# Attention and a two-layer feed-forward block on one core: output weights in 8 KB runs, a stepped weight load, one reciprocal DMA a head, WI in four pieces

## The chip, the core and the metric

The kernel runs on one core of a Trainium2 chip. The metric is device time in microseconds (us): the median of three runs. A separate execution was profiled; all rows of the profile come from that one. Engines are named as in the profile: PE (matrix multiply) with PEld (its weight loads), DVE (vector), ACT (activation), POOL (GpSimd), SP (which issues most DMAs here). SPq is SP's instruction queue; POOL issues DMAs too, those that convert from float32 to float16.

## The reference

Eight batches, eight heads, 576 positions, head dimension 64. Each head has a coarse attention over means of four positions and a local attention over positions less than four apart; their sum goes through a feed-forward block of 512 to 2048 to 512 with an ELU between.

```python
q_d, k_d, v_d = (t.reshape(B, H, Sd, 4, D).mean(axis=3) for t in (q, k, v))
out_up = np.repeat(sm_attn(q_d, k_d, v_d), 4, axis=2)
mask = np.abs(pos[:, None] - pos[None, :]) < 4
...                                      # softmax of the masked scores
out_local = np.matmul(attn, v)
attn_out = out_up + out_local
...
x = attn_out.transpose(0, 2, 1, 3).reshape(B * S, H * D)      # 4608 x 512
h = x @ w_in                                                  # w_in 512 x 2048
g = np.where(h > 0.0, h, np.exp(np.minimum(h, 0.0)) - 1.0)
out = g @ w_out                                               # w_out 2048 x 512
```

## The kernel before

**Attention.** The heads go in pairs, so that two heads of 64 fill 128 partitions; there are four pairs a batch, index `j`. For each pair PE transposes q and k, makes local scores in six blocks of 96 positions and coarse scores beside them; ACT takes the exponential into a tile `pex`; POOL casts v to float16 (line 226). `outputs` (line 536) multiplies by v into a PSUM tile `lg`. `normalise` has DVE multiply `lg` by the reciprocals of the softmax sums, `rcb`, into `ln` (line 554 in batches 0 to 2; lines 558 and 561 after that), and adds the local part and the coarse part, repeated four times, into `xt`: the transposed input of the feed-forward block, 512 tokens a tile. Most of these additions are POOL's (line 574).

**Reciprocals.** For batches 1 to 7, `denominators(b)` collects all softmax sums of a batch in one PSUM bank: 32 rows for each pair `j`, of which ten are used. A matmul with a window of the constant `IND` as its weights chooses the row; the windows start at column `a`. Before, rows 0 to 3 hold the local sums of the pair's first head, 144 positions a row, rows 4 to 7 those of its second head, row 8 the coarse sums of the first and row 9 of the second. DVE takes the reciprocal into `rc`. Each reciprocal is then needed on 64 partitions. In batches 1 and 2 (`spread_four`) PE does that, with the constant `FOUR`. In batches 3 to 7 `spread_out` writes `rc` to a DRAM tile `rd`, and `spread_in` (line 466) reads it back with a step of zero over 64 partitions: for each head `e` one DMA of the local part (4 x 144 numbers a pair) and one of the coarse part (144), four a batch, on SP's queue.

**Feed-forward.** `WI` holds w_in as 128 partitions x 4 blocks of rows x 2048 columns, `WO` holds w_out as 128 x 16 x 512. For a token tile `t` and a block `fc` of 128 of the 2048 hidden units, `mm1` (line 592) makes `hp` with four matmuls, each with 128 columns of WI as weights and 512 tokens moving. ACT takes the exponential (line 597), DVE finishes the ELU in two steps (`e`, line 598; `gt`, line 601). `mm2` (line 615) uses `gt` as weights and WO as the moving operand, sums over all 16 blocks, and ACT copies the result out (line 621). In `mm1` and `mm2` there are nine token tiles, 16 steps each, four matmuls a step. The first two blocks of the first tile are made ahead of that by `ahead` (line 793), as soon as each pair of heads is done.

**Loads.** WI comes in five DMAs on POOL's queue (`load_wi`, line 138): columns 0 to 256, 256 to 512, and then 512 at a time. WO comes in four DMAs of four row blocks (`load_wo`, line 142); a row of w_out is 2 KB in DRAM and 1 KB once converted. POOL also issues q and k of batches 0 and 1 (line 152). SP issues v (line 204), and q and k of later batches (line 170).

**Order.** Nothing is scheduled automatically. Every step is put into a list with a planned time by `at`, the list is sorted, and the steps are emitted in that order; each engine works its own steps off in that order, waiting where an operand is not there. The times of the front are in the table `F` (planned times of the WI loads: `wi`), those of later batches in `PLAN`, `LATER` and `LAST`. POOL's order in the front therefore interleaves DMA issues, casts of v, and additions into `xt`.

Of the kernel before, what the change touches and what calls it, by code (L numbers as in the profile page):

```python
# [15 lines left out]
B, H, S, D = 8, 8, 576, 64  # L16
SD = S // 4
# [9 lines left out]
NPAIR = H // 2  # L27
RW = S + SD
# [5 lines left out]
I1 = 31  # L34
# [34 lines left out]
def _free(ap: bass.AP, dims) -> bass.AP:  # L69

    return bass.AP(tensor=ap.tensor, offset=ap.offset, ap=[list(ap.ap[0])] + [list(d) for d in dims])
# [3 lines left out]
def kernel(  # L75
# [9 lines left out]
    nc = tc.nc  # L85
# [26 lines left out]
    def bank(tag, name):  # L112
        pool = late["ps"] if tag == "hp" else ps
        return pool.tile([128, 512], FP32, tag=tag, bufs=2, name=name)
# [16 lines left out]
    C = {}  # L131
    WI = sb.tile([128, DMC, DFF], FP16, tag="WI", bufs=1, name="WI")
    WO = sb.tile([128, FCN, DM], FP16, tag="WO", bufs=1, name="WO")
    KT = [sb.tile([128, S + 2 * KO], FP16, tag=f"kt{i}", bufs=1, name="kt") for i in range(3)]

    def load_wi(a, z):
        src = moe_w_in.rearrange("(c p) m -> p c m", p=128)[:, :, a:z]
        nc.gpsimd.dma_start(out=WI[:, :, a:z], in_=src)

    def load_wo(n):  # L140
        src = moe_w_out.rearrange("(c p) m -> p c m", p=128)[:, 4 * n : 4 * n + 4, :]
        nc.gpsimd.dma_start(out=WO[:, 4 * n : 4 * n + 4, :], in_=src)

    KD = [sb.tile([128, 2 * KG + 16], FP16, tag=f"kd{i}", bufs=1, name="kd") for i in range(3)]
# [270 lines left out]
    def local(b, j, e, g, a, n):  # L415
        return st[(b, j)]["p"][:, e, g, a : a + n]

    def far(b, j, e, kg, a, n):
        return st[(b, j)]["p"][0:KG, e, kg, HB + a : HB + a + n]
# [11 lines left out]
    def denominators(b):  # L431


        den = bank("hp" if b < 3 else "misc", "den")
        for r in range(8):
            a = 126 if r == 0 else I1 - r
            for j in range(NPAIR):
                nc.tensor.matmul(
                    den[32 * j : 32 * j + 32, 0:SD], C["IND"][:, a : a + 32],
                    local(b, j, r // 4, r // 2 % 2, SD * (r % 2), SD),  # L440
                    start=(r == 0), stop=False, tile_position=(0, 32 * j),
                )
        for e in range(2):
            a = 63 + I1 - 8 - e
            for kg in range(2):
                for j in range(NPAIR):
                    nc.tensor.matmul(
                        den[32 * j : 32 * j + 32, 0:SD], C["IND"][0:KG, a : a + 32],
                        far(b, j, e, kg, 0, SD), start=False,
                        stop=(e == 1 and kg == 1), tile_position=(0, 32 * j),  # L450
                    )
        rc = RC[b] = sb.tile([128, SD], FP16, tag="rc", bufs=1, name="rc")
        nc.vector.reciprocal(out=rc[:], in_=den[:, 0:SD])
# [7 lines left out]
    def spread_in(b):  # L461
        rd = RD[b]
        rcb = RB[b] = sb.tile([128, NPAIR, RW], FP16, tag="rcb", bufs=2, name="rcb")
        for e in range(2):
            for r, a, n in ((4 * e, 0, S), (8 + e, S, SD)):
                nc.sync.dma_start(
                    out=rcb[64 * e : 64 * e + 64, :, a : a + n],
                    in_=bass.AP(
                        tensor=rd.tensor, offset=rd.offset + r * SD,
                        ap=[[0, 64], [32 * SD, NPAIR], [1, n]],  # L470
                    ),
                )


    def den_pair(b, j, den):
# [48 lines left out]
    xts = {}  # L524
# [59 lines left out]
    def mm1(t, fc):  # L584
        if fc == 0:
            gts[t] = sb.tile([128, FCN, TBLK], FP16, tag="gt", bufs=2, name="gt")
        if t == 0 and fc < 2:
            hp = FS.pop(fc)[:]
        else:
            hp = bank("misc" if t == 0 and fc % 2 else "hp", "hp")[:]  # L590
            for dc in range(DMC):
                nc.tensor.matmul(  # L592
                    hp, WI[:, dc, 128 * fc : 128 * fc + 128], xts[t][:, dc, :],
                    start=(dc == 0), stop=(dc == DMC - 1),
                )
        e = sb.tile([128, TBLK], FP16, tag="e", bufs=3, name="e")
        nc.scalar.activation(out=e[:], in_=hp, func=AF.Exp)  # L597
        nc.vector.tensor_scalar(  # L598
            out=e[:], in0=e[:], scalar1=1.0, scalar2=-1.0, op0=AB.min, op1=AB.add
        )  # L600
        nc.vector.scalar_tensor_tensor(  # L601
            out=gts[t][:, fc, :], in0=hp, scalar=0.0, op0=AB.max, in1=e[:], op1=AB.add
        )
# [24 lines left out]
    Z = fs.tile([128, 512], FP16, tag="Z", bufs=1, name="Z")  # L628
# [96 lines left out]
    def selections(name):  # L725

        if name == "SEL":
            t = C[name] = sb.tile([KW, 1280], FP16, tag=name, bufs=1, name=name)
            src, parts = C["ID"], ((0, 6, 0), (6, 4, 32))
            step = 64  # L730
        else:
            src = sb.tile([KW, 10], FP16, tag="I4", bufs=1, name="I4")
            nc.vector.tensor_reduce(
                out=src[:], in_=_free(C["ID"][:, 0:1], [[1, 10], [32, NPAIR]]), axis=AX.X, op=AB.add
            )
            t = C[name] = sb.tile([KW, 640], FP16, tag=name, bufs=1, name=name)
            parts, step = ((0, 4, 0), (4, 1, 8)), None
        for n, m, col in parts:
            nc.gpsimd.tensor_copy(
                out=t[:, 128 * n : 128 * n + 128 * m].rearrange("p (n e d) -> p n e d", e=2, d=64),  # L740
                in_=_free(src[:, col : col + 1], [[1, m], [step or (4 if m > 1 else 1), 2], [0, 64]]),
            )

    FS = {}
# [43 lines left out]
    def ahead(dc):  # L788

        for fc in range(2):  # L790
            if dc == 0:
                FS[fc] = bank("hp", "hp")
            nc.tensor.matmul(
                FS[fc][:], WI[:, dc, 128 * fc : 128 * fc + 128],
                xts[0][:, dc, :], start=(dc == 0), stop=(dc == 3),
            )

# [6 lines left out]
    def at(time, fn, *args):  # L804
        events.append((time, len(events), fn, args))
# [30 lines left out]

    at(-100, first)
    at(-65.22, second)
    F = dict(T=[-39.33, -39.15, -31.04, -21.56], S=[-39.11, -32.34, -29.72, -11.12], Z=[-38.51, -29.77, -26.1, -10.33], C=[-30.42, -27.74, -25.81, -9.49], V=[-12.6, -10.91, -10.66, -8.84], P=[-20.39, -13.26, -9.3, -7.53], O=[-10.7, -10.4, -9.52, -5.16], N=[-9.74, -9.71, -7.85, -0.84], H=[-8.39, -5.24, -0.57, -0.51], lv=[-32.55, -28.19, -28, -27.16], cv=[-27.16, -11.94, -11.66, -10.33], lw=[-11.12, -10.26, -8.16, 0.45], rp=[-40.13, -31.28, -14.21, -9.89], D=[-27.94, -26.42, -12.68, -9.32], wi=[-30.86, -13.56, -10.44, -4.62, 0.11], cf=[-9.53], k=[-39.29, -38.62, -33.61, -32.56, -31.33])
    FK = dict(Tq=[0, 0, 0, 0], Tk=[3, 0, 0, 0], S=[2, 0, 0, 1], Z=[0, 0, 0, 1], P=[0, 0, 0, 0], O=[0, 0, 1, 1], D=[0, 0, 0, 1])  # L840
    for j in range(NPAIR):
        at(F["T"][j], first_transposes, j, (FK["Tq"][j], FK["Tk"][j]))
        at(F["S"][j], first_scores, j, 0, FK["S"][j])
        at(F["Z"][j], first_scores, j, 1, FK["Z"][j])
        at(F["D"][j], first_dens, j, FK["D"][j])
        at(F["V"][j], first_v, j)
        at(F["P"][j], first_spread, j, FK["P"][j])
        at(F["O"][j], first_outputs, j, FK["O"][j])
        at(F["N"][j], first_normalise, j)
        at(F["H"][j], ahead, j)  # L850
        at(F["lv"][j], load_v, 0, j)
        at(F["cv"][j], cast_v, 0, j)
        at(F["lw"][j], load_v, 1, j)
        at(F["rp"][j], run_pair, 1, j)
    for x, a, z in zip(F["wi"], (0, 256, 512, 1024, 1536), (256, 512, 1024, 1536, 2048)):
        at(x, load_wi, a, z)
    at(F["cf"][0], close_front)
    late_consts = (("VR", vr_np), ("IND", ind_np), ("SEL", None), ("QI", qi_np), ("FOUR", None))
    for x, (name, a) in zip(F["k"], late_consts):
        if a is None:  # L860
            at(x, selections, name)
        else:
            at(x, const, a, name, nc.sync)
# [9 lines left out]
    def mm1_at(t, i):  # L873
        a, d = MM1[t] if t < 4 else (MM1[3][0] + 16 * (t - 3), 1)
        return a + d * i
# [19 lines left out]
    for b in range(4, B):  # L895
        z = mm1_at(b, 0)
        PLAN[b] = {k: [z + x for x in a] for k, a in (LATER if b < B - 1 else LAST).items()}
    for b in range(1, B):
        p = PLAN[b]
        for j in range(NPAIR):  # L900
            n = NPAIR * (b - 2) + j
# [28 lines left out]
    for n, x in enumerate([-3.64, 3.75, 7.34, 13.63]):  # L930
        at(x, load_wo, n)
    for t in range(NT):
        for i in range(16):
            at(mm1_at(t, i), mm1, t, i)
            if 16 * t + i <= 16 * NT - 4:
                at(mm2_at(t, i), mm2, t, i)
# [32 lines left out]
```

## Time and profile before

| | us |
|---|---|
| median of 3 runs | 371.23 |
| lowest and highest of them | 369.82, 371.39 |
| the profiled execution | 368.46 |
| its span, first to last instruction | 366.7 |
| PE busy | 343.6 |
| DVE busy | 244.2 |
| ACT busy | 201.0 |
| POOL busy | 146.7 |

The mean granted TensorE clock is 0.986 of full speed. DMA moved 49.15 MB in 132,099 packets, of which 7,664 (6.26 MB, 11.3% of the time of 16 DMA engines) came from POOL's software queue and 123,946 (41.93 MB, 52.6%) from SP's hardware queue. A row of a group gives the line, engine, operation, tiles and shapes, the number of instructions, then busy us and mean ns of one, then the idle time of the engine just before them and what ended it. PE's and PEld's rows overlap: a matmul's length in a group includes its way through the array, so the distance of one start from the next is shorter.

### The profile page before, as it was taken

What the parts mean: (1) busy time and instruction counts of PE and PEld (TensorE: products, weight loads), DVE (VectorE), ACT (ScalarE), POOL (GpSimd) and SP (SyncE); (2) the same over time, 40 slices, a digit from 0 to 9 for tenths busy, and PEclk for the clock granted to TensorE, in tenths of its full rate; (3) what the DMA queues carried; (4) which work ended last, traced back from release to release, by engine and by line L of the source; (5) the groups of instructions that cost most, each with busy time, mean ns of one, the idle gap of its engine ahead of it and who ended that gap; (6) DMA issues with size and microseconds to landing.
All of it is one profiled execution on the core that took longest, in us unless ns stands there. A gap on an engine that the chain in (4) does not pass through costs nothing.

```text
span 366.7 us, 8593 instructions
## 1 busy us (share of the span) xinstructions
PE 343.6 (94%) x3432; PEld 177.6 (48%) x3432; DVE 244.2 (67%) x451; ACT 201.0 (55%) x321; POOL 146.7 (40%) x264
## 2 busy tenths in 40 slices
PE   6995989999789999999999989999999999999996
PEld 3773444544444455455445444544454444444443
DVE  2059478756777777987799779868865865555510
ACT  3854586357963764667367736773664344344321
POOL 8296363399437912780297029703500410000000
PEclk9999699999998999999999999999999999999999
DMA  9999968999995869497949594914103101001012
GB/s 173 210 172 195 171 101 163 217 236 265 227 156 120 173 158 198 46 229 172 206 109 221 142 217 104 229 45 105 47 30 95 49 29 59 29 29 59 29 57 88
DMA packets 132099, 49.15 MB, mean 134 GB/s; under 512 B 116875, under 2 KB 127579, under 8 KB 132059
## 3 DMA queue, kind: packets, MB, share of 16 engines
q1 hardware_dynamic: 123946, 41.93, 52.6%
q0 software_dynamic: 7664, 6.26, 11.3%
q8 instruction: 27, 0.44, 0.5%
q10 hardware_dynamic: 448, 0.40, 0.4%
q14 instruction: 14, 0.11, 0.1%
HBM read 42.27 MB, written 9.62 MB: 142 GB/s over the span
## 4 chain that ended last, share of the span: by engine, by line
PE 66%; DVE 10%; DMA 8%; issue 6%; POOL 4%; ACT 4%; SPq 1%; ACTq 0%; DVEq 0%; POOLq 0%
PE op L615 28%; PE hp L592 26%; DMA v<-in_v_dram 3%; DVE ln L561 3%; DMA rcb<-rd 2%; PE sc L390 2%; DVE e L598 2%; DVE gt L601 2%; ACT pex L410 2%; DMA R<-Rc 2%; PE lg L536 2%; PE tq L260 1%; PE sc L400 1%; DMA rd<-rc 1%; POOL t L332 1%
## 5 line engine op out<-in xcount | busy, mean ns | idle before, releaser
L592 PE MATMUL hp<-xt,WI 128*128 128x512 f16 x568 | 148.3, 385 | 5.4 <-DVE gt L601 2.6
L615 PE MATMUL op<-WO,gt 128*128 128x512 f16 (+2 forms) x592 | 145.4, 374 | 0.0
L597 ACT ACTIVATE e<-hp 128x512 f16<-128x512 f32 x144 | 86.1, 599 | 104.0 <-PE hp L592 100.3
L601 DVE SCALAR_TENSOR_TENSOR gt<-hp,e 128x512 f16<-128x512 f32 x144 | 99.6, 692 | 5.4
L598 DVE TENSOR_SCALAR e<-e 128x512 f16<-128x512 f16 x144 | 61.3, 426 | 50.8 <-ACT e L597 50.4
L615 PEld LDWEIGHTS <-gt 128*128 128x128 f16 x592 | 54.9, 98 | 61.9 <-issue 0.5
L574 POOL TENSOR_TENSOR xt<-ln 128x64 f16<-128x64 f16 (+8 forms) x68 | 40.1, 618 | 111.7 <-DVE ln L561 95.9
L592 PEld LDWEIGHTS <-WI 128*128 128x128 f16 x568 | 52.7, 98 | 66.0 <-issue 6.6
L410 ACT ACTIVATE pex<-sc 112x864 f16<-112x864 f32 (+2 forms) x72 | 54.8, 808 | 12.9 <-PE sc L400 11.7
L427 DVE TENSOR_TENSOR pex<-pex,MASK 112x1152 f16<-112x1152 f16 x27 | 21.7, 804 | 18.8 <-ACT pex L410 18.8
L621 ACT COPY os<-op 128x512 f32<-128x512 f32 (+2 forms) x37 | 21.2, 574 | 19.6 <-PE op L615 19.2
L226 POOL CAST v<-v 112x768 f16<-112x768 f32 x32 | 26.3, 828 | 9.2 <-DMA v<-in_v_dram 9.1
L189 POOL CAST q<-q 96x768 f16<-96x768 f32 x24 | 22.2, 925 | 6.5 <-DMA q<-in_q_dram 6.3
L189 POOL CAST k<-k 96x768 f16<-96x768 f32 x24 | 20.1, 839 | 4.1 <-DMA k<-in_k_dram 4.0
L291 ACT CAST qt<-tq 128x720 f16<-128x720 f32 x24 | 18.3, 761 | 5.4 <-PE tq L260 5.4
L536 PE MATMUL lg<-pex,v 112*64 112x96 f16 x384 | 14.3, 213 | 2.6 <-DVE ln L561 1.6
L390 PEld LDWEIGHTS <-kt 64*112 64x112 f16 x324 | 10.5, 127 | 12.6 <-issue 8.9
L536 PEld LDWEIGHTS <-v 112*64 112x64 f16 x384 | 10.8, 112 | 10.8 <-issue 5.9
L390 PE MATMUL sc<-qt,kt 64*112 64x96 f16 x324 | 14.0, 218 | 1.2 <-DVE ln L554 0.8
L561 DVE TENSOR_TENSOR ln<-lg,rcb 128x576 f16<-128x576 f32 x20 | 15.0, 748 | 0.0
L326 DVE TENSOR_REDUCE kd<-kt 128x144 f16<-128x576 f16 x20 | 14.9, 743 | 0.0
L260 PEld LDWEIGHTS <-q 96*128 96x128 f16 x144 | 9.6, 97 | 5.9 <-issue 1.0
(110 smaller groups left out, 251.5 us busy)
## 6 DMA issues: line engine op xcount, KB each, us to landing
v<-in_v_dram SPq DMA_DIRECT2D x30, 336.0 KB, 5.6
out_dram<-os SPq DMA_DIRECT2D x35, 256.0 KB, 2.0
q<-in_q_dram SPq DMA_DIRECT2D x25, 288.0 KB, 3.9
k<-in_k_dram SPq DMA_DIRECT2D x24, 288.0 KB, 4.7
rcb<-rd SPq DMA_DIRECT2D x10, 288.0 KB, 4.4
WO<-in_moe_w_out_dram POOLq DMA_DIRECT2D x4, 512.0 KB, 5.9
WI<-in_moe_w_in_dram POOLq DMA_DIRECT2D x3, 512.0 KB, 8.9
q<-in_q_dram POOLq DMA_DIRECT2D x7, 144.0 KB, 6.7
```

The lines of the kernel that those rows point to most:

```text
L189: nc.gpsimd.tensor_copy(out=x[:], in_=t[:].rearrange("p (e c) d -> p c e d", e=2))
L226: nc.gpsimd.tensor_copy(out=v16[:], in_=v32[:].rearrange("p (e c) d -> p c e d", e=2))
L390: nc.tensor.matmul(sc[e][0:KW, a : a + QB], s["kt"][r, KO - PAD + QB * c :][:, 0:KW], s["qt"][c][r], start=True, stop=True,)
L410: nc.scalar.activation(out=s["p"][0:rows, e, :, a : a + n], in_=g2(sc[0:rows], a, n), func=AF.Exp, scale=SCALE / 16 if b == 1 and a == HB ...
L536: nc.tensor.matmul(lg[64 * e : 64 * e + 64, a : a + QB], v16[:, c, e, :], local(b, j, e, c // 3, QB * (c % 3), QB), start=True, stop=True,)
L561: nc.vector.tensor_tensor(out=h2(ln[:, 0:S]), in0=g2(lg[:], 0, HB), in1=h2(rcb[:, j, 0:S]), op=AB.mult)
L574: eng.tensor_tensor(out=xt(t)[:, j, t0 - TBLK * t : t1 - TBLK * t], in0=ln[:, la : la + z - a], in1=_rep4(ln[:, ga : ga + (z - a) // 4]), ...
L592: nc.tensor.matmul(hp, WI[:, dc, 128 * fc : 128 * fc + 128], xts[t][:, dc, :], start=(dc == 0), stop=(dc == DMC - 1),)
L597: nc.scalar.activation(out=e[:], in_=hp, func=AF.Exp)
L598: nc.vector.tensor_scalar(out=e[:], in0=e[:], scalar1=1.0, scalar2=-1.0, op0=AB.min, op1=AB.add)
L601: nc.vector.scalar_tensor_tensor(out=gts[t][:, fc, :], in0=hp, scalar=0.0, op0=AB.max, in1=e[:], op1=AB.add)
L615: nc.tensor.matmul(op_[:, a:z], gts[t][:, fc, 128 * tt : 128 * tt + 128], WO[:, fc, a:z], start=(fc == 0), stop=(fc == FCN - 1),)
```

## The change

Three things are changed together.

- **WO in runs of 8 KB.** Each load of WO takes 512 consecutive rows of w_out, and each partition now gets four consecutive rows of them, one run of 8 KB in DRAM, in place of rows 128 apart. Hidden unit 512 n + 4 p + c is now on partition p of block 4 n + c. For `gt` to agree with that, `mm1` makes block `fc` from every fourth column of WI: the weights of its matmuls are 128 columns with a step of four (8 bytes). A block needs all of 512 columns to have arrived, so the first two pieces of WI become one, and the later of their two planned times goes.
- **One DMA a head for the reciprocals.** The rows of the sums are put in another order: rows 0 to 3 local and row 4 coarse for the first head, rows 5 to 9 for the second. A head's 720 numbers are then contiguous in `rd`, and `spread_in` reads them with one DMA a head. The windows of `IND` change to suit.
- **FOUR** is built for the new order of rows, with one copy in place of two.

```diff
+    def w_in(dc, fc):
+
+        a = 512 * (fc // 4) + fc % 4
+        return WI[:, dc, a : a + 509 : 4]
+
...
     def load_wo(n):
-        src = moe_w_out.rearrange("(c p) m -> p c m", p=128)[:, 4 * n : 4 * n + 4, :]
+        src = moe_w_out[512 * n : 512 * n + 512].rearrange("(p c) m -> p c m", c=4)
         nc.gpsimd.dma_start(out=WO[:, 4 * n : 4 * n + 4, :], in_=src)
...
         for r in range(8):
-            a = 126 if r == 0 else I1 - r
+            a = 126 if r == 0 else I1 - r - r // 4
...
         for e in range(2):
-            a = 63 + I1 - 8 - e
+            a = 59 + I1 - 5 * e
...
         for e in range(2):
-            for r, a, n in ((4 * e, 0, S), (8 + e, S, SD)):
-                nc.sync.dma_start(
-                    out=rcb[64 * e : 64 * e + 64, :, a : a + n],
-                    in_=bass.AP(
-                        tensor=rd.tensor, offset=rd.offset + r * SD,
-                        ap=[[0, 64], [32 * SD, NPAIR], [1, n]],
-                    ),
-                )
+            nc.sync.dma_start(
+                out=rcb[64 * e : 64 * e + 64, :, :],
+                in_=bass.AP(
+                    tensor=rd.tensor, offset=rd.offset + e * RW,
+                    ap=[[0, 64], [32 * SD, NPAIR], [1, RW]],
+                ),
+            )
...
-                    hp, WI[:, dc, 128 * fc : 128 * fc + 128], xts[t][:, dc, :],
+                    hp, w_in(dc, fc), xts[t][:, dc, :],
...
-            parts, step = ((0, 4, 0), (4, 1, 8)), None
+            parts, step = ((0, 5, 0),), 5
...
-                in_=_free(src[:, col : col + 1], [[1, m], [step or (4 if m > 1 else 1), 2], [0, 64]]),
+                in_=_free(src[:, col : col + 1], [[1, m], [step, 2], [0, 64]]),
...
-                FS[fc][:], WI[:, dc, 128 * fc : 128 * fc + 128],
+                FS[fc][:], w_in(dc, fc),
...
-    F = dict(..., wi=[-30.86, -13.56, -10.44, -4.62, 0.11], ...)
+    F = dict(..., wi=[-30.86, -10.44, -4.62, 0.11], ...)
...
-    for x, a, z in zip(F["wi"], (0, 256, 512, 1024, 1536), (256, 512, 1024, 1536, 2048)):
+    for x, a, z in zip(F["wi"], (0, 512, 1024, 1536), (512, 1024, 1536, 2048)):
         at(x, load_wi, a, z)
```

More of the change, by code (lines that the diff above doesn't have):

```diff
@@ L838 @@
     at(-65.22, second)
-    F = dict(T=[-39.33, -39.15, -31.04, -21.56], S=[-39.11, -32.34, -29.72, -11.12], Z=[-38.51, -29.77, -26.1, -10.33], C=[-30.42, -27.74, -25.81, -9.49], V=[-12.6, -10.91, -10.66, -8.84], P=[-20.39, -13.26, -9.3, -7.53], O=[-10.7, -10.4, -9.52, -5.16], N=[-9.74, -9.71, -7.85, -0.84], H=[-8.39, -5.24, -0.57, -0.51], lv=[-32.55, -28.19, -28, -27.16], cv=[-27.16, -11.94, -11.66, -10.33], lw=[-11.12, -10.26, -8.16, 0.45], rp=[-40.13, -31.28, -14.21, -9.89], D=[-27.94, -26.42, -12.68, -9.32], wi=[-30.86, -13.56, -10.44, -4.62, 0.11], cf=[-9.53], k=[-39.29, -38.62, -33.61, -32.56, -31.33])
+    F = dict(T=[-39.33, -39.15, -31.04, -21.56], S=[-39.11, -32.34, -29.72, -11.12], Z=[-38.51, -29.77, -26.1, -10.33], C=[-30.42, -27.74, -25.81, -9.49], V=[-12.6, -10.91, -10.66, -8.84], P=[-20.39, -13.26, -9.3, -7.53], O=[-10.7, -10.4, -9.52, -5.16], N=[-9.74, -9.71, -7.85, -0.84], H=[-8.39, -5.24, -0.57, -0.51], lv=[-32.55, -28.19, -28, -27.16], cv=[-27.16, -11.94, -11.66, -10.33], lw=[-11.12, -10.26, -8.16, 0.45], rp=[-40.13, -31.28, -14.21, -9.89], D=[-27.94, -26.42, -12.68, -9.32], wi=[-30.86, -10.44, -4.62, 0.11], cf=[-9.53], k=[-39.29, -38.62, -33.61, -32.56, -31.33])
     FK = dict(Tq=[0, 0, 0, 0], Tk=[3, 0, 0, 0], S=[2, 0, 0, 1], Z=[0, 0, 0, 1], P=[0, 0, 0, 0], O=[0, 0, 1, 1], D=[0, 0, 0, 1])
```

## The prediction

> **What bounds the kernel now.** I began with the page's busy times, its slices and its groups. A quoted row of a timeline or chain begins with its start and its length in us.
>
> ```profile
> PE 343.6 (94%) x3432; PEld 177.6 (48%) x3432; DVE 244.2 (67%) x451; ACT 201.0 (55%) x321; POOL 146.7 (40%) x264
> ...
> L592 PE MATMUL hp<-xt,WI 128*128 128x512 f16 x568 | 148.3, 385 | 5.4 <-DVE gt L601 2.6
> L615 PE MATMUL op<-WO,gt 128*128 128x512 f16 (+2 forms) x592 | 145.4, 374 | 0.0
> ```
>
> PE is the bound, and two lines of matmuls are most of it. A microsecond comes off the span only if PE stops waiting, runs slowly for less time, or issues less; the change issues no matmul less. So I looked for the places where PE waits close to what is edited. The windows at the end of batches 3, 4, 5, 6 and 7 (length, then PE busy, PEld busy, and so on) show this:
>
> ```profile
> 136.00:148.00 12.00, 12.00 (x125) 6.07 (x124) 9.86 (x19) 5.24 (x9) 2.65 (x4) 1.00 1.01 175
> 178.00:184.00 6.00, 5.69 (x82) 3.12 (x82) 5.06 (x12) 1.78 (x3) 2.73 (x5) 1.00 1.17 231
> 214.00:220.00 6.00, 5.01 (x79) 2.72 (x73) 4.42 (x9) 1.41 (x3) 2.65 (x4) 1.00 1.29 229
> 250.00:256.00 6.00, 5.69 (x82) 2.98 (x80) 4.95 (x10) 1.83 (x4) 2.64 (x4) 1.00 0.23 70
> 285.00:296.00 11.00, 9.84 (x75) 4.59 (x74) 8.95 (x17) 3.57 (x6) 5.28 (x8) 1.00 0.15 52
> ```
>
> In batch 3 PE is busy throughout; in the other four it misses 0.31, 0.99, 0.31 and 1.16, 2.77 us together. DVE's waits after 130 us, and the chain of waits around 210 us, say why:
>
> ```profile
> DVE ln L558 <- DMA rcb<-rd: 4.7, 4, 1.5
> ```
>
> ```profile
> 207.36 2.35 DMA rd<-rc
> ...
> 209.73 0.61 SPq L466
> ...
> 210.39 0.60 SPq L466
> ...
> 211.05 0.61 SPq L466
> ...
> 211.70 4.40 DMA rcb<-rd
> ```
>
> The reciprocals go out to DRAM and come back in four DMAs that SP issues one after the other, 0.66 us apart. DVE waits for the last (0.87, 1.55, 0.81 and 1.50 us in batches 4 to 7, none in batch 3), the normalisation is late, and PE lacks a free bank. The last place is the front, in the timeline at 33 to 38 us:
>
> ```profile
> 34.30 0.79 POOL L138 DMA_DIRECT2D WI<-in_moe_w_in_dram  x1
> 34.64 1.44 DVE L598 TENSOR_SCALAR e<-e 128x512 f16<-128x512 f16 x1
> 35.09 0.84 POOL L226 CAST v<-v 112x768 f16<-112x768 f32 x1
> 36.86 1.44 PE L592 MATMUL hp<-xt,WI 128*128 128x512 f16 x3 [2.38 <-DVE v L201]
> ```
>
> An `e` step that takes 0.29 elsewhere takes 1.44 and ends just behind a POOL cast; PE idles 2.38 us. The windows give a granted clock of 0.77 from 34 to 37 us and 0.55 from 37 to 43: 3.0 x 0.46 + 6.0 x 0.90 = 6.8 us at half clock, 3.4 us of work lost.
>
> **One DMA a head.** It removes two of four issues on SP. The second and last then goes at 210.39 instead of 211.70: 1.31 us sooner. Its size is 360 KB; the page has 4.4 us to landing for 288 KB and 4.0 for 72 KB, so 4.5 for this one. It lands at 214.9 instead of 216.10, 1.2 us sooner, and the four waits shrink from 4.73 to about 0.35 + 0.30 = 0.65. PE gets back between nothing and 2.77 us; as batch 3 without a wait shows no idle PE, I take the share of the wait that goes, 2.77 x 4.1 / 4.73 = **2.4 us**. What is late next is the two normalisations in a row (0.30 + 0.75 us each), already in these windows. SP's key transposes and the q, k and v loads behind them move up by 1.3 us; nobody waits for them there: nothing. The matmuls of `denominators` change only the columns of IND they read, and FOUR is filled in one copy instead of two (0.84 us for both at 7.95), ahead of loads that PE does not wait for: at most 0.2, taken as nothing.
>
> **WO in four rows a partition.** Four loads of 2048 packets in all become 512 of four times the size, if a packet is a run. POOL's issue takes 0.78 us for 512 rows (WI, WO) and 0.63 for 192 (q, k), so about 0.60 for 128. Three of the four have no one waiting behind them; the one at 45.06 stands before a cast that stretches a DVE step (0.97 for 0.29 at 45.93): 0 to 0.18, I take 0.1. PE never waits for WO (0.0 idle at L615). Without that cover, a late last piece (issued 56.27, landed 6.1 us later, first product of WO at 61.67) would cost at most its landing.
>
> **WI in four pieces.** POOL loses a DMA of 0.78 us at 19.88, and the first piece becomes 512 KB instead of 256. Its first reader is PE at 28.22, while 512 KB pieces land 8.9 us after an issue at 9.98: nothing. What shifts is v. If v of batch 1 lands sooner, since 0.26 MB of WI no longer goes out just before its issue at 23.21, POOL's second cast is over before the step at 34.64 and 1.44 - 0.29 = 1.15 us go. If v of batch 0 lands later instead, about 1 us is lost (the second rival). Between -1.15 and +1.0 I take **-0.4**, leaning to the gain, as POOL has 0.78 us less in its queue either way.
>
> **Every fourth column.** All 576 weight loads of mm1 step 8 bytes instead of 2; the trace has no such load. Three shapes of PEld (last figure before the wait: mean ns):
>
> ```profile
> L592 PEld LDWEIGHTS <-WI 128*128 128x128 f16 x568 | 52.7, 98 | 66.0 <-issue 6.6 <-DVE gt L601 2.2
> L390 PEld LDWEIGHTS <-kt 64*112 64x112 f16 x324 | 10.5, 127 | 12.6 <-issue 8.9 <-ACT kt L304 1.7 <-ACT e L597 1.3
> L438 PEld LDWEIGHTS <-IND 112*32 112x32 f16 x224 | 4.1, 96 | 1.1 <-issue 1.1
> ```
>
> From 32 to 112 columns a load grows by (127 - 96) / 80 = 0.39 ns a column, so 128 would take 133; the full-width load takes 98, a shortcut that a step might lose. In the chain of waits four matmuls take 0.86 us, 216 ns each, with a load under each; so a load has 118 ns to spare. Of the 568 loads, 520 lie under a 512-column matmul and 48 follow a short one of the attention, where a longer load shows in full. Lower bound: no change (a load faster than 98 has no reason). Shortcut lost: 48 x 35 ns = 1.7 us. Upper bound: without its columns the 32-column load has 96 - 32 x 0.39 = 84 ns; with every column four times as long, 84 + 128 x 0.39 x 4 = 284 ns, so 520 x 68 ns + 48 x 186 ns = 44 us. The nearest row is the 98 ns of the same shape, so I take 0.
>
> [...]
>
> **Sum.** 2.4 + 0.1 + 0.4 = 2.9 us. The profiled execution took 368.46 (span 366.7 and 1.8 around it), so it would take 365.6. The median of the runs, 371.23, is 2.8 us above it, so I forecast 371.23 - 2.9 = **368.3**. About 0.5%, 1.86 us, is what a measurement of this kernel can tell from no change.
>
> **The rivals.**
> (1) Slower: the strided load outgrows the matmul. It decides once PEld of L592 exceeds 216 ns. Twice the column cost (184 ns) stays below it; three times (234) gives 520 x 18 + 48 x 136 ns = 16 us, four times 44: 384 to 412, say 385. For it: no row shows a step. Against: 118 ns to spare. 0.14.
> (2) The load grows to 130 to 190 ns and shows only behind short matmuls: +1.5 to +4.4, eating the gain: 371. 0.12.
> (3) Slower: v comes later in the front. By the page a software packet takes 0.113 x 366.7 x 16 / 7664 = 87 ns and one of SP's hardware queue 0.526 x 366.7 x 16 / 123946 = 25; a v load is 1344 rows, 84 per DMA engine, and 84 x (87 + 25) = 9.4 us is close to the 10.0 and 9.6 that v needs beside WI, against 4.7 almost alone: the queues take turns. The first piece's 32 packets per engine grow from about 55 to 109 ns (87 ns for a mean of 817 bytes, scaled), so v of batch 0 lands 32 x 54 ns = 1.7 us later; less POOL's 0.78, about 1 us through POOL's casts (waiting 7.10 us for v at 17.85), the adds at 25.84 and the DVE step that waits for them at 28.95. If PE's idling then costs one more such stretch of half clock: 371.23 - 2.5 + 1.0 + 3.4 = 373.1. Against: slack behind two of the casts. 0.13.
> [...]
> (4) The front gains more: the stall goes and PE is busy early enough to keep its clock: 371.23 - 2.5 - 1.15 - 3.4 = 364.2. 0.10.
> (5) It does not do what it says: rcb lands when it did, as two larger DMAs take as long as four: 370.7. 0.06.
>
> **How the numbers follow.** The forecast has 0.45, of which 0.38 lies over 0.5% faster and 0.07 within. Faster 0.38 + 0.10 = 0.48. Within 0.07 + 0.09 of (2) + 0.06 = 0.22. Slower 0.14 + 0.13 + 0.03 of (2) = 0.30. The range reaches from (4), 364.0, past (3) to 374.5, leaving out (1) and a little at the ends. Both signs are in it; the forecast's own range is 366.5 to 370.
>
> **What would show it.** Right: PEld of L592 near 98 ns and four of its matmuls still 0.86 us; ten rcb DMAs in place of twenty, DVE's wait for rcb under 1 us, PE idle before L536 near zero after 133 us; the DVE step near 34.6 us at 0.3. Wrong: PEld of L592 over 216; PE reaching its first matmul of WO later than 61.67; half clock where there was none; rcb landing over 5 us after issue.

## The result

| | us |
|---|---|
| before, median of 6 runs on the same chip | 370.52 (365.78 to 371.66) |
| after, median of 6 runs | 378.02 (376.30 to 382.42) |
| after / before, with its 95% interval | 1.0261 [1.0205, 1.0316] |
| the profiled execution of after, and its span | 382.42, 380.6 |

The change makes the kernel 2.6% slower, where 0.8% faster was forecast. Each ratio in this document leaves out the executions, of either kernel, that fell into a slower state with a lower clock, so it is not the quotient of the two medians; the profiled execution of after is one of them (mean clock 0.946 where the other five have 0.959 to 0.973 and spans of 374.5 to 378.6), so its rows overstate the loss by some 4 us. The waits shown below stand in the program, and so in all six.

The page of after has these rows in answer to those of before:

```profile
PE 353.3 (93%) x3432; PEld 190.7 (50%) x3432; DVE 243.9 (64%) x451; ACT 201.4 (53%) x321; POOL 145.2 (38%) x262
...
PEclk9965558999998999999999999999999999999999
...
L596 PE MATMUL hp<-xt,WI 128*128 128x512 f16 x568 | 150.1, 388 | 8.0 <-DMA WI<-in_moe_w_in_dram 4.4
L619 PE MATMUL op<-WO,gt 128*128 128x512 f16 (+2 forms) x592 | 145.3, 374 | 0.0
```

The matmuls of mm1 (L596, L592 before) are hardly longer, 388 ns for 385. But the idle time ahead of them is now ended mostly by a DMA of WI, where before's row had DVE's `gt`, and three slices of the clock (9.5 us each) stand at 5. All of it is in the front: PE starts its first matmul of WO at 76.88 us, where before it was 61.67, so 15.2 us are lost by then and 1.3 won back after it.

The windows of 20 us show how much work is missing (start and end, length, busy us of PE, PEld, DVE, ACT and POOL, then the granted clock, DMA share, GB/s). Of before:

```profile
20.00:40.00 20.00, 15.50 (x294) 9.33 (x289) 15.07 (x29) 9.48 (x18) 12.59 (x20) 0.89 1.18 189
40.00:60.00 20.00, 17.63 (x239) 9.18 (x238) 12.89 (x28) 15.30 (x29) 10.38 (x17) 0.94 0.70 115
```

Of after:

```profile
20.00:40.00 20.00, 16.01 (x243) 10.16 (x239) 9.69 (x20) 5.09 (x10) 10.35 (x17) 0.57 0.78 134
40.00:60.00 20.00, 11.73 (x73) 5.13 (x74) 6.52 (x13) 6.81 (x13) 5.03 (x8) 0.50 0.53 92
```

In after, four matmuls of mm1 take 1.83 us to the next start at a clock of 0.50 (52.68 to 54.51) and 0.95 at 1.00 (152.24 to 153.19), so busy time times clock is taken as work at full speed: 15.50 x 0.89 + 17.63 x 0.94 = 30.4 us before, 16.01 x 0.57 + 11.73 x 0.50 = 15.0 after. The 15.4 us between them are the loss. PE is idle for 12.3 of the 40 us where it was idle for 6.9 before, which is 5.4 of it; the other 10.0 are the lower clock (busy time times what the clock lacks of full speed: 12.8 us, 2.8 before). PE and the DMA engines are both less busy in the second window: neither has too much to do, they wait for one another. The chain of waits of after names the circle (start, length, what):

```profile
36.00 0.87 PE hp L797 x2
36.86 0.29 issue
37.15 5.45 DMA WI<-in_moe_w_in_dram
42.60 0.05 issue
42.65 1.91 PE hp L797 x4
44.56 0.29 issue
44.85 5.96 DMA WI<-in_moe_w_in_dram
50.81 0.05 issue
50.86 1.47 PE hp L596 x3
```

PE's matmuls release a load of WI, its landing releases PE's next matmuls, and so again. POOL's timeline has the first half of this (in brackets: idle before, and what ended it):

```profile
37.15 0.80 POOL L143 DMA_DIRECT2D WI<-in_moe_w_in_dram  x1 [1.35 <-PE hp L797]
...
44.85 0.79 POOL L143 DMA_DIRECT2D WI<-in_moe_w_in_dram  x1 [5.04 <-PE hp L797]
```

PE's timeline has the other half:

```profile
42.65 1.90 PE L797 MATMUL hp<-xt,WI 128*128 128x512 f16 x4 [3.56 <-DMA WI<-in_moe_w_in_dram]
...
45.86 0.59 PE L596 MATMUL hp<-xt,WI 128*128 128x512 f16 x1 [0.59 <-DVE v L206]
50.86 1.47 PE L596 MATMUL hp<-xt,WI 128*128 128x512 f16 x3 [4.41 <-DMA WI<-in_moe_w_in_dram]
```

None of these four waits is needed: `ahead` (L797, blocks 0 and 1) and the matmuls at L596 that follow (block 2) read columns 0 to 511, whose load was issued at 9.77 us and landed 11.4 us later, and POOL is loading columns 1024 to 1535 and 1536 to 2047. In the traces none of before's five WI issues waits for PE; after's third and fourth do, 1.35 and 5.04 us. The step is what differs: as one tile, `WI[:, dc, a : a + 509 : 4]` seems to be taken to overlap columns that it does not touch, for a load waits for readers of other pieces (those 1.35 and 5.04 us), and readers for the load (3.56 and 4.41 us). The trace would fit a comparison by first and last element alone, the author's guess, which no run tests: of block 2's four matmuls the one on row block 0, which lies in the tile ahead of all that the load writes, starts at 45.86 without it, and the three on row blocks 1 to 3 wait for it.

The batch ends, where the reciprocals were to gain, have these windows (14.2 us later than before's):

```profile
150.20:162.20 12.00, 12.00 (x125) 6.38 (x123) 9.82 (x20) 5.58 (x9) 2.65 (x4) 1.00 0.80 175
192.20:198.20 6.00, 5.69 (x81) 3.11 (x80) 4.88 (x10) 1.79 (x4) 2.65 (x4) 1.00 1.24 235
228.20:234.20 6.00, 5.38 (x81) 3.01 (x80) 4.69 (x10) 1.43 (x4) 2.65 (x4) 1.00 1.27 246
264.20:270.20 6.00, 5.93 (x82) 3.10 (x80) 5.12 (x11) 1.98 (x4) 2.65 (x4) 1.00 0.17 54
299.20:310.20 11.00, 10.11 (x74) 5.03 (x74) 9.21 (x17) 3.57 (x6) 5.29 (x8) 1.00 0.13 49
```

PE misses 0.31 + 0.62 + 0.07 + 0.89 = 1.89 us in the last four, 2.77 before. DVE's waits and the chain say why it is not less (total us, times, longest):

```profile
DVE ln L562 <- DMA rcb<-rd: 3.9, 4, 1.2
```

```profile
221.96 2.37 DMA rd<-rc
...
224.35 0.61 SPq L470
...
225.01 5.33 DMA rcb<-rd
```

One issue stands between `rd` and the last `rcb` instead of three, but that last DMA, of 360 KB where before's last had the 72 KB of a coarse part, takes 5.33 us to land instead of 4.40. From the first issue to the landing it is 5.99 us (224.35 to 230.34), 6.37 before (209.73 to 216.10).

### The profile page after: what moved, and what is told of

The parts are those of the page before. It is cut to its first block, busy times and chain, and to the rows that moved or that the text cites. A ratio compares the mean times of both kernels' runs of the same rounds, so it can differ in the third digit from the quotient of the medians.

```text
span 380.6 us, 8576 instructions
## 1 busy us (share of the span) xinstructions
PE 353.3 (93%) x3432; PEld 190.7 (50%) x3432; DVE 243.9 (64%) x451; ACT 201.4 (53%) x321; POOL 145.2 (38%) x262
## 4 chain that ended last, share of the span: by engine, by line
PE 60%; DVE 11%; DMA 9%; ACT 4%; issue 4%; POOL 2%; SPq 1%; DVEq 0%; ACTq 0%; POOLq 0%
PE op L619 25%; PE hp L596 24%; DMA rcb<-rd 4%; DMA WI<-in_moe_w_in_dram 3%; DVE ln L565 3%; DVE e L602 2%; DVE gt L605 2%; ACT pex L415 2%; PE sc L395 2%; DMA rd<-rc 2%; PE tq L265 1%; PE lg L540 1%; ACT e L601 1%; DVE pex L432 1%; DVE ln L558 1%
## 5 line engine op out<-in xcount | busy, mean ns | idle before, releaser
L596 PE MATMUL hp<-xt,WI 128*128 128x512 f16 x568 | 150.1, 388 | 8.0 <-DMA WI<-in_moe_w_in_dram 4.4
L596 PEld LDWEIGHTS <-WI 128*128 128x128 f16 x568 | 61.4, 115 | 63.8 <-DMA WI<-in_moe_w_in_dram 5.5
L194 POOL CAST q<-q 96x768 f16<-96x768 f32 x24 | 21.1, 879 | 5.8 <-DVE rcb L525 5.8
L540 PE MATMUL lg<-pex,v 112*64 112x96 f16 x384 | 15.1, 220 | 2.0 <-ACT rcb L525 1.0
L540 PEld LDWEIGHTS <-v 112*64 112x64 f16 x384 | 11.4, 117 | 10.9 <-issue 6.9
L395 PE MATMUL sc<-qt,kt 64*112 64x96 f16 x324 | 14.2, 221 | 0.4 <-ACT kt L309 0.3
```

Of the source, the lines that this page charges most:

```text
L194: nc.gpsimd.tensor_copy(out=x[:], in_=t[:].rearrange("p (e c) d -> p c e d", e=2))
L395: nc.tensor.matmul(sc[e][0:KW, a : a + QB], s["kt"][r, KO - PAD + QB * c :][:, 0:KW], s["qt"][c][r], start=True, stop=True,)
L540: nc.tensor.matmul(lg[64 * e : 64 * e + 64, a : a + QB], v16[:, c, e, :], local(b, j, e, c // 3, QB * (c % 3), QB), start=True, stop=True,)
L596: nc.tensor.matmul(hp, w_in(dc, fc), xts[t][:, dc, :], start=(dc == 0), stop=(dc == DMC - 1),)
```

## The experiments

The question of each group stands ahead of it. A ratio is that of the kernel's time to before's on the same chip, with its 95% interval.

### Does the step alone do it, and is it the tile?

**The stepped weights and the four pieces, put into the kernel before; nothing else.**

```diff
-                    hp, WI[:, dc, 128 * fc : 128 * fc + 128], xts[t][:, dc, :],
+                    hp, w_in(dc, fc), xts[t][:, dc, :],
...
-    for x, a, z in zip(F["wi"], (0, 256, 512, 1024, 1536), (256, 512, 1024, 1536, 2048)):
+    for x, a, z in zip(F["wi"], (0, 512, 1024, 1536), (512, 1024, 1536, 2048)):
```

> The kernel before with stepped weights and WI in four pieces of one tile; WO loaded as before (so the hidden units of gt and of WO are paired in another order) and the reciprocals as before. Theory A: the false waits are all here, 375-380 (ratio 1.01-1.03), POOL waits for PE at WI loads, PE waits for WI. Theory B: also slow, as the first piece is as big: 374-378. Theory C: 2-3 us over before at most.

Measured: 381.18 us, ratio 1.0331 [1.0248, 1.0415], first matmul of WO at 76.78 us. The whole loss comes with these two edits. Its POOL timeline has the same waits for PE, 1.35 and 4.86 us, at 37.16 and 44.86.

**The whole change, with WI as four tiles of 512 columns.**

```diff
-    WI = sb.tile([128, DMC, DFF], FP16, tag="WI", bufs=1, name="WI")
+    WI = [sb.tile([128, DMC, 512], FP16, tag=f"WI{n}", bufs=1, name="WI") for n in range(4)]
...
-        a = 512 * (fc // 4) + fc % 4
-        return WI[:, dc, a : a + 509 : 4]
+        return WI[fc // 4][:, dc, fc % 4 : fc % 4 + 509 : 4]
...
-        nc.gpsimd.dma_start(out=WI[:, :, a:z], in_=src)
+        nc.gpsimd.dma_start(out=WI[a // 512][:], in_=src)
```

> The whole change, but WI is four tiles of 512 columns instead of one tile of 2048, so a load of one piece and a stepped read of another can't be taken to overlap. Theory A (waits): the stepped reads made POOL's third and fourth WI loads wait for PE and PE wait for them; with four tiles PE has no wait for WI in the front, no 42.65 or 50.86 us matmul, and the time falls from 378 to 366-370 (ratio to before 0.985-1.0). Theory B (the bigger first piece delays v, and the clock falls): the v casts stay late, half clock stays long, time 374-378 (1.01-1.02). Theory C (weight loads of 114 ns): no change from the changed kernel, 376-378. PEld of mm1 stays at 114 ns under all three.

Measured: 367.96 us, ratio 0.9987 [0.9937, 1.0037]. The loads, their sizes and their order, the step and the matmuls are those of after. POOL's waits for PE, 6.4 us in after, are gone from the trace, the first matmul of WO starts at 61.21, and the windows are back where before's were:

```profile
20.00:40.00 20.00, 15.92 (x306) 10.95 (x306) 13.28 (x27) 8.61 (x15) 12.65 (x20) 0.91 1.03 178
40.00:60.00 20.00, 17.11 (x242) 9.48 (x241) 14.51 (x30) 16.64 (x33) 9.65 (x17) 1.00 0.73 126
```

This settles the cause: the loss comes with one tile that is read with a step, and with the waits that follow from it, not with the step itself, the runs of WO or the size of the pieces.

**The whole change, one tile, but contiguous weights.**

```diff
-        return WI[:, dc, a : a + 509 : 4]
+        return WI[:, dc, 128 * fc : 128 * fc + 128]
```

> The whole change in one tile of WI, but mm1 takes 128 neighbouring columns as before (so the hidden units of gt and of WO are paired in another order). Only the step differs from the changed kernel. Theory A: the tracking of contiguous reads is exact, no false wait, as e1 or up to 1 us better: ratio to before 0.990-1.003. Theory B (first piece and WO): as slow as the changed kernel, 1.015-1.03. PEld of mm1 back to 98 ns.

Measured: 368.00 us, ratio 0.9942 [0.9901, 0.9982], first matmul of WO at 62.30, no load of WI that waits for PE. It is the counterproof: with the tile kept and the step taken out the loss goes as well. Both are needed for it. Its windows also tell what the waits do to the clock:

```profile
20.00:40.00 20.00, 17.16 (x262) 10.55 (x261) 12.15 (x25) 7.61 (x14) 12.09 (x19) 0.66 1.03 177
40.00:60.00 20.00, 17.47 (x246) 9.03 (x245) 14.69 (x31) 16.00 (x33) 9.64 (x17) 1.00 0.68 115
```

Its granted clock is 0.50 from 25 to 35 us, as in after, though no wait of this kind exists here; but from 40 us on it is 1.00, where after stays at 0.50 to 60. So the early half clock is not the work of the false waits, and the first matmul of WO is late by only 0.63 us with it; the half clock of the second window is theirs.

**One tile and the step kept, the last three loads issued before the first reader.** If POOL's waits were all, moving the loads ahead of the reads would remove the loss.

```diff
-    F = dict(..., wi=[-30.86, -10.44, -4.62, 0.11], ...)
+    F = dict(..., wi=[-30.86, -10.44, -10.43, -10.42], ...)
```

> The changed kernel with WI's last three loads planned one behind the other before the first reader. POOL then has no reader to wait for; what remains of theory A is PE's side: the second row block of the first stepped read waits for all of WI to land (about 33-36 us instead of 28). Time between e1 and the changed kernel: ratio 1.00-1.015. If POOL's waits weren't the costly ones: as the changed kernel, 1.02-1.03.

Measured: 373.26 us, ratio 1.0156 [1.0086, 1.0225], first matmul of WO at 71.69. POOL waits for PE no longer, but three pieces of WI now go out just ahead of a v load, and its timeline shows what that costs:

```profile
23.21 2.26 POOL L143 DMA_DIRECT2D WI<-in_moe_w_in_dram  x3
37.36 0.83 POOL L231 CAST v<-v 112x768 f16<-112x768 f32 x1 [11.90 <-DMA v<-in_v_dram]
...
39.49 3.49 POOL L578 TENSOR_TENSOR xt<-ln 128x288 f16<-128x288 f16 x7
```

The cast of v waits 11.90 us, the additions into `xt` queue behind it on POOL, and PE waits for those (2.24 us at 40.77). So one false wait was traded for a true one: the experiment tells only that the loads cannot simply go earlier. Its 71.69 is not all due to that either: the profiled execution took 378.13 us, the other five 372.69 to 374.16, and its clock is 0.50 already from 10 to 25 us, ahead of those three loads.

### What do the other parts do by themselves?

**WI in four pieces alone, contiguous weights.**

```diff
-    F = dict(..., wi=[-30.86, -13.56, -10.44, -4.62, 0.11], ...)
+    F = dict(..., wi=[-30.86, -10.44, -4.62, 0.11], ...)
...
-    for x, a, z in zip(F["wi"], (0, 256, 512, 1024, 1536), (256, 512, 1024, 1536, 2048)):
+    for x, a, z in zip(F["wi"], (0, 512, 1024, 1536), (512, 1024, 1536, 2048)):
```

> The kernel before with WI in four pieces alone: contiguous weights, WO and reciprocals as before. Theory A: no new wait, within 1% of before (368-373; ratio 0.993-1.007). Theory B: v of batch 0 lands 1-2 us later, PE idles near 21 us, a long stretch of half clock, 374-377 (1.01-1.02). Theory C: as before.

Measured: 370.89 us, ratio 1.0058 [1.0008, 1.0109], first matmul of WO at 64.01. Three casts of v from POOL's timeline of this kernel:

```profile
14.81 0.83 POOL L226 CAST v<-v 112x768 f16<-112x768 f32 x1 [4.08 <-DMA v<-in_v_dram]
...
20.00 0.83 POOL L226 CAST v<-v 112x768 f16<-112x768 f32 x1 [3.15 <-DMA v<-in_v_dram]
...
23.89 0.83 POOL L226 CAST v<-v 112x768 f16<-112x768 f32 x1 [3.06 <-DMA v<-in_v_dram]
```

And of before:

```profile
17.85 0.83 POOL L226 CAST v<-v 112x768 f16<-112x768 f32 x1 [7.10 <-DMA v<-in_v_dram]
...
20.64 1.61 POOL L226 CAST v<-v 112x768 f16<-112x768 f32 x2
```

The first comes sooner, but the third starts at 23.89 instead of 21.4 and has a wait of its own for v. The granted clock from 20 to 30 us is 0.64, 1.00 before. By this pair it looks like the prediction's rival (3), at about +2.1 us (0.0058 x 368). But the kernel above with contiguous weights in one tile has the same first piece, a third cast at 22.93, a clock of 0.70 from 20 to 30 us, and a ratio of 0.9942, so that these are what costs the 0.6% is not shown.

**The reciprocals alone, one DMA a head.**

```diff
-            for r, a, n in ((4 * e, 0, S), (8 + e, S, SD)):
...
+            nc.sync.dma_start(
+                out=rcb[64 * e : 64 * e + 64, :, :],
```

> The kernel before with the reciprocals' part alone (new order of rows, one DMA a head, FOUR in one copy). All theories: the prediction's term was -2.4 us (ratio 0.9935), with the wait of DVE for rcb falling from 4.7 to about 0.65 us. The changed kernel's trace has landings of 5.3 us instead of 4.5 and 3.9 us of waits left, so a theory that the larger DMA eats the gain expects -0.3 to -1.0 us (0.997-1.0).

Measured: 366.90 us, ratio 0.9969 [0.9923, 1.0015]. DVE's wait after 130 us:

```profile
DVE ln L557 <- DMA rcb<-rd: 3.7, 4, 1.2
```

4.7 to 3.7 us, not to 0.65. PE's waits for `ln` (1.6 to 0.7) and for `gt` at mm1 (1.8 to 1.5) go from 3.4 to 2.2 us together. That 1.2 us is what the part can be seen to gain; the ratio, 1.1 us less with an interval from -2.8 to +0.6, agrees with it and does not prove it.

**WO in runs of 8 KB alone**, all else as before.

```diff
-        src = moe_w_out.rearrange("(c p) m -> p c m", p=128)[:, 4 * n : 4 * n + 4, :]
+        src = moe_w_out[512 * n : 512 * n + 512].rearrange("(p c) m -> p c m", c=4)
```

> The kernel before with WO in four rows a partition and nothing else (hidden units paired in another order). The prediction's term was -0.1 us: ratio 0.995-1.005, WO's software packets a quarter as many, the POOL issue 0.57 instead of 0.78 us.

Measured: 366.47 us, ratio 0.9947 [0.9908, 0.9986]; 6128 packets in POOL's software queue instead of 7664, an issue of WO takes 0.55 to 0.58 us (0.76 to 0.79 before). Some 2 us, more than the 0.1 forecast. No row names the wait that went: the profile has its first matmul of WO at 60.82, 0.85 sooner than before's, which is less than what single executions of one kernel differ by (the spans of this one lie between 363.0 and 367.5). Where the rest comes from stays open.

### Can the cost of the first piece be taken out of the four tiles?

**Four tiles, the first piece in two DMAs by its rows, at the two times of before.**

```diff
+        c0, c1 = {0: (0, 2), 1: (2, 4)}.get(a, (0, 4))
+        a -= a % 2
...
+        nc.gpsimd.dma_start(out=WI[a // 512][:, c0:c1, :], in_=src)
...
```

> Four tiles as in e1, and WI's first 512 columns come in two DMAs again, split by row blocks (0-1 and 2-3), the second at the old planned time of the second piece, so that v is met by 256 KB instead of 512. Theory A (waits) with e3's finding that the big first piece costs about 0.6%: 1 to 3 us less than e1, ratio to before 0.985-0.997. Theory D (the rest of the missing gain is the stepped load or WO): no better than e1, 0.996-1.004.

Measured: 367.56 us, ratio 0.9985 [0.9941, 1.0029]: as the four tiles without it. Its casts of v stand at 14.53, 19.05, 21.24 and 25.79, its first matmul of WO at 63.44.

**Four tiles, the first piece later** (planned at -20 instead of -30.86, and issued at 17.24 us, behind the first cast of v at 16.47, where it was 9.77); and the same with contiguous weights, to price the step.

```diff
-    F = dict(..., wi=[-30.86, -10.44, -4.62, 0.11], ...)
+    F = dict(..., wi=[-20, -10.44, -4.62, 0.11], ...)
```

> Four tiles as in e1, and the first piece of WI planned behind the first cast of v (-20 in place of -30.86), so that v of batch 0 meets less of it. If v's lateness in the front is what eats the gain of e1: ratio to before 0.985-0.995. If not: 0.996-1.003. Its first reader is PE near 28 us; should the piece land later than that, PE waits and the ratio is over 1.

Measured: 368.94 us, ratio 0.9998 [0.9951, 1.0044].

```diff
-        return WI[fc // 4][:, dc, fc % 4 : fc % 4 + 509 : 4]
+        return WI[fc // 4][:, dc, 128 * (fc % 4) : 128 * (fc % 4) + 128]
```

> As e9, but mm1 takes neighbouring columns (hidden units of gt and of WO paired in another order). The only difference from e9 is the step of the weights, 98 against 114 ns. If the longer load lies under the matmuls everywhere: the same as e9 within 0.3%. If it shows at the 48 loads behind short matmuls: 0.8 us, 0.2% below e9, hardly to be told; 0.5% or more below would need another cost of the step.

Measured: 368.26 us, ratio 0.9974 [0.9931, 1.0016]. Neither placing of the first piece gains anything; the step costs 0.24% in this pair, with intervals that overlap, so its own price is not told apart from nothing. The pair above, four stepped tiles against one tile without the step, points the same way with 0.45%, and its intervals overlap too.

**The parts that seemed to gain, put together without the four pieces:** WO in runs of 4 KB, a step of 4 bytes, the five pieces of before as five tiles, one DMA a head.

```diff
-        a = 512 * (fc // 4) + fc % 4
-        return WI[:, dc, a : a + 509 : 4]
+        n, c = (fc // 2, 0) if fc < 4 else (1 + fc // 4, 256 * (fc % 4 // 2))
+        c += fc % 2
+        return WI[n][:, dc, c : c + 255 : 2]
...
-        src = moe_w_out[512 * n : 512 * n + 512].rearrange("(p c) m -> p c m", c=4)
+        src = moe_w_out[512 * n : 512 * n + 512].rearrange("(g p c) m -> p g c m", g=2, c=2)
```

> WO with two rows a partition (runs of 4 KB), mm1's weights from every second column (a step of 4 bytes), WI in the five pieces of before as five tiles of their own, and one DMA a head for the reciprocals. Theory: the four pieces cost what they measured alone (+0.6%) because the larger first piece puts v of batch 0 back; with the five pieces that cost is gone and the casts of v stand at 14.8, 20.6 and 20.6 us as before; the reciprocals bring their 0.3% and half the WO packets saved bring about half of its 0.5%. Packets of the software queue fall from 7664 to about 6640. PEld of mm1 is between 98 and 114 ns. First matmul of WO at 61 to 62 us, ratio about 0.994. Rival: the gains of WO and of the reciprocals do not add up with five tiles, or the four pieces were never what held the four tiles back: then it measures as the four tiles did, 0.9987. Second rival: the later WO and WI loads meet the same v loads whatever their runs, and only fewer packets by three quarters help: 0.997, the reciprocals alone.

Measured: 368.04 us, ratio 1.0012 [0.9974, 1.0050]. The theory, 0.994, lies outside the interval; the packets came out as expected (6640), the gains did not add up. In the profiled execution the casts of v are at 14.43, 18.82, 21.18 and 24.98, near those of the kernel with the first piece in two by rows, and not at before's 17.85, 20.64 and 21.4; the clock from 20 to 40 us is 0.66 and the first matmul of WO is at 64.66. So, by this one profile, five pieces do not by themselves keep v where it was, and the shares of half a per cent above can't simply be added.

### What does a stepped weight load take?

**Four tiles become two of 1024 columns, with every eighth column as weights (16 bytes).**

```diff
+        return WI[fc // 8][:, dc, fc % 8 : fc % 8 + 1017 : 8]
...
+        src = moe_w_out[1024 * h : 1024 * h + 1024].rearrange("(p c) m -> p c m", c=8)[:, c : c + 4, :]
```

> WI in two tiles of 1024 columns, mm1 from every eighth column (16 bytes), WO in eight rows a partition, four loads as before; WI's four loads planned before the first reader, so the time itself says little. What counts is PEld of mm1 after 140 us. [...]

Measured: 373.71 us in one run. The groups by shape from 140 to 340 us (last figure before the wait: mean ns of one) with a step of 2 bytes, the whole change unstepped:

```profile
L595 PEld LDWEIGHTS <-WI 128*128 128x128 f16 x388 | 36.5, 98 | 44.9 <-DVE gt L604 2.1 <-issue 1.2
```

Of 4 bytes, the kernel with two rows a partition:

```profile
L597 PEld LDWEIGHTS <-WI 128*128 128x128 f16 x387 | 36.4, 98 | 44.8 <-DVE gt L606 2.2 <-issue 1.2
```

Of 8 bytes, the four tiles:

```profile
L595 PEld LDWEIGHTS <-WI 128*128 128x128 f16 x387 | 42.4, 114 | 40.4 <-DVE gt L604 2.1 <-issue 1.1
```

Of 16 bytes:

```profile
L596 PEld LDWEIGHTS <-WI 128*128 128x128 f16 x384 | 53.6, 145 | 32.0 <-DVE gt L605 2.1 <-issue 0.7
```

Behind matmuls of 512 columns, four matmuls of mm1 still take 0.86 us in the chain with a step of 16 bytes: the load is hidden there with all four steps. Behind a short matmul of the attention what it takes over 98 ns shows. From the first of four to the next start it is 0.87 us with a step of 2 bytes (182.12 to 182.99 in before, 61.43 to 62.30 in the whole change unstepped), 0.89 with 8 (193.43 to 194.32 in after) and 0.92 with 16 (65.91 to 66.83). The one time is not a price of the step: the first matmul of WO is at 66.83, 5.6 us later than with four tiles, and the loads of WI go out at other places too; from there on the kernel takes 305.1 us, as the others do.

## Why the prediction was wrong

**The step that failed is "Every fourth column", together with "WI in four pieces".** The prediction priced the step by the length of a weight load, and the pieces by their bytes and issues. It never asked which waits the program gets when a slice of the tile changes its shape, though the loads of WI stand in POOL's queue beside their readers in `ahead`. The 0.4 us forecast as a gain for the pieces, with bounds of -1.15 and +1.0, and the 0 for the step, became a loss of 15.2 us before the first matmul of WO in the profiled execution, and of 9.6 us by the ratio (0.0261 x 368). No rival named it. The range, to 374.5, ended below every run of after. Three of the signs that were named as "wrong" did come: the first matmul of WO later than 61.67 (76.88), half clock where there was none, and `rcb` landing over 5 us after its issue (5.33).

Of the waits of 3.56 and 4.41 us, 7.1 us fall between 40 and 60 us, where PE is idle for 8.3 us in all (2.4 before); the rest of that window's loss is its clock, 0.50 throughout. The trace has half clock after both waits, but it does not show them bring it down, since the clock was at 0.50 from 25 us on, and POOL's first wait for PE begins at 35.80. What it shows, beside the kernel with contiguous weights, is that with the waits the clock does not come back (0.50 from 40 to 60, 1.00 there). What makes the early fall stays open: of the kernels with the large first piece, after and the one with contiguous weights have it (0.57 and 0.66 from 20 to 40 us), and the four tiles do not (0.91).

**The length of the load was right in its main bound, wrong in its details.** 118 ns to spare were enough: 114 ns, and rivals (1) and (2), 0.26 together, fell. That loads behind short matmuls show "in full" is what the runs have: for four matmuls there 0.02 us more at 114 ns than at 98, and 0.05 more at 145. For 48 loads this is by estimate 48 x 16 ns = 0.8 us, where the forecast had 0; it is less than the ratios tell apart. The 133 ns for a lost shortcut, drawn from the 32- and 112-column loads, is the length of none of them: 98 ns with a step of 4 bytes, 114 with 8, 145 with 16. Why it is 98 up to 4 bytes and more from 8 on no run shows.

**The reciprocals were over-sized.** The mechanism is right and the term was 2.4 us; the runs show about 1 (2.77 to 1.89 us of idle PE in the windows of after, 3.4 to 2.2 us of waits in the kernel with that part alone). What failed is "so 4.5 for this one": the rows of 288 KB in 4.4 us and 72 KB in 4.0 were carried on as a line, and 360 KB took 5.3 us. The two DMAs of 360 KB are in flight together (issued at 224.35 and 225.01, landed by 230.34) and bring as many bytes as the four did, so most of the 1.31 us of the issues is given back in the landing; that sharing is why a 360 KB DMA takes longer here is not shown by a run. This is close to rival (5), which had 0.06.

**Rival (3) may be real, but it is not where the loss was.** The four pieces alone measure +0.6% [0.1, 1.1], about 2 us where the rival had 1.0 + 3.4, and one pair of profiles shows a later v and half clock with it. Its 9.4 us for a load of v, and the queues that take turns in it, are the prediction's estimate: the trace has 10.0 and 9.6 us beside WI and 4.7 almost alone, and no run tests the turns. **WO** was forecast at -0.1 us and measures -2 us alone [-3.4, -0.5], for a reason that no row shows.

**Taking what the program orders apart from what the hardware does,** the sum was too hopeful by 0.7%, not by 3.4: with four tiles the kernel stands at -0.1% [-0.6, +0.4], and the forecast was -0.8%. Without the step, in one tile, it is -0.6% [-1.0, -0.2].

## What to carry to other kernels

Before an access pattern is changed, list who else touches that tile, and ask how the waits are derived: here, with a stepped slice of a tile that is loaded in pieces, loads waited for readers of other pieces (1.35 and 5.04 us) and the readers for the loads (3.56 and 4.41 us). Give each piece that is loaded by itself a tile of its own; here that was worth 2.7%. In the trace it showed as a DMA issue that waits for the engine that reads its tile, followed by that engine waiting for the DMA, while both get less busy.

## What the runs showed of the hardware

- The full-width weight load takes 98, 98, 114 and 145 ns with steps of 2, 4, 8 and 16 bytes, that is with 128 weights spread over 0.25, 0.5, 1 and 2 KB a partition. From 0.5 KB on this is 31 ns a KB over 83, and it does not fall below 98. Behind a matmul of 512 columns, 216 ns, all of it is hidden; behind a short one four matmuls take 0.87, 0.89 and 0.92 us with loads of 98, 114 and 145 ns. These are lengths of the profile's records; in no run did they show in the kernel's time.
- From the first matmul of WO to the end, the profiled executions of all fourteen kernels take between 302.5 and 305.8 us, whatever their edits; the start of that matmul lies between 57.86 and 76.88. What these fourteen differ in lies in the front:

| kernel | first matmul of WO, us | span less that, us | clock 20 to 60 us |
|---|---|---|---|
| before | 61.67 | 305.0 | 0.91 |
| after | 76.88 | 303.7 | 0.53 |
| stepped weights and four pieces alone | 76.78 | 305.8 | 0.53 |
| one tile, loads early | 71.69 | 304.7 | 0.80 |
| four pieces alone | 64.01 | 305.2 | 0.83 |
| four tiles | 61.21 | 304.7 | 0.96 |
| reciprocals alone | 57.86 | 304.5 | 1.00 |

- The last row's front of 57.86 us stands beside a time that is hardly better than before's, and its edit has only the building of FOUR in the front; single profiles of these kernels differ in the front by almost 4 us without a cause that the edit shows. What is less than that was read here from the waits and the ratios, not from the spans. No version was clearly faster than the kernel before and kept the pairing of hidden units.
